# One-hots with four token columns side by side, a third place for x, stores issued ahead of loads

## The chip, the cores and the metric

The kernel runs on one core of one Trainium2 chip. The metric is the device time of one execution in microseconds (us), as the median of several runs. Of one execution there is a profile as well, taken by the hardware profiler. PE is TensorE's matmul, PEld its weight load, DVE is VectorE, ACT is ScalarE, POOL is GpSimd and SP is SyncE, which here only issues DMAs.

## What is computed

The reference has two parts. The first is a causal convolution over 8 batches of 3584 tokens with 192 features, 8 heads of 24 features and 7 taps per head (taps through a softmax). The second is a mixture of 8 experts on its result, 28672 tokens in all:

```
skip_score = x @ w_skip;  do_compute = skip_score > 0;  out = x.copy()
xc = x[do_compute];  logits = xc @ w_gate;  e_idx = argmax(logits)
gate_w = softmax(logits) at e_idx
for e in range(E):  h = max(xc[e_idx == e] @ w1[e], 0);  y = gate_w * (h @ w2[e])
out[do_compute] = xc + y
```

`w1[e]` is 192 x 1024, `w2[e]` is 1024 x 192.

## The kernel before, in words

**Stage 1: convolution and routing, by batch.** A batch is cut into 30 columns of 120 tokens (`NC = 30`, `R = 120`). `load_x(b)` fetches its 30 columns with 8 tokens of overlap into `xs`, 128 partitions wide, with three DMAs (four or more for the first two batches). `conv_head` (L331 to L340) makes one head: two matmuls of `toep` (the banded taps) with 15 columns of `xs` each into `pc`, which ACT copies into `ys` (L339). `pc` has two buffers, so two heads can run ahead of ACT. `ys` has two buffers too, by turns of the batches, and `store_y` writes it to `out`. `xs` has two buffers: even batches in one, odd ones in the other.

While batch b is convolved, batch b-1 is routed: `router` transposes `ys` on PE (`tp`, L423, copied by ACT to `ya`), multiplies with the router's weights (`pl`, `pb`) and leaves logits `lg`; `slots` finds on DVE the expert (`oh`), and by a matmul `pr` (L518) and a scan the slot of each token in its expert's list, as a row `rf` (0 to 127) and a column `qf` of a list of 128 x 144. Then `invert` (L575 on) turns slots into lists of tokens: for each column of 120 tokens it makes two one-hot matrices, `oa` (120 x 128, row of the slot, L606, times the column's token number `vtab`, L611) and `ob` (120 x 144, column of the slot, L617), and PE adds their product to `inv` (L589). DVE makes eight columns with one instruction each of `oa`, the product with `vtab`, and `ob`, so 30 columns are groups of 8, 8, 8 and 6. Before, `oa` is laid out `[R, P, IC]`, with the eight token columns innermost, and `ob` is `[R, IC, NQ]`, with the 144 list columns innermost and `qf` repeated along them.

**The weights of experts 0 and 1** are prepared in the same stage, as a background generator `split_weights`: 7 loads into `raw` (`w1` in one piece of 128 rows and two of 64, `w2` in four), 7 reductions on DVE for the largest value (`am`, L260), a scale, then 7 scalings on ACT to fp16 (`wt`, L279) and 7 subtractions on DVE for the low half (`wt`, L290). That is 26 steps an expert. `raw` has one buffer.

**What sets the order.** The order of instructions on each engine is the order in which the program writes them, and each engine and SP's queue handle theirs in that order; a scheduler moves nothing. In `phase1_step(b)` the eight heads are written one after another, and behind each head a table says how much else follows: `RR` steps of routing, `IR` steps of the inversion, `BGS[b][h]` steps of the background. Expert 0's steps are queued at batch 0, expert 1's at batch `E1`. After the last head comes `load_x(b + 2)`, and then `store_y(b)`. A load of `xs` waits until PE has finished with the batch that used the buffer; a copy into `ys` waits until the store of two batches ago has landed.

**Stage 2: the experts.** From the end of batch 7 on, blocks of 256 tokens are gathered from `out`, scaled, multiplied by `w1` (`ph`, L815), made into a high and low fp16 half (`hh` on ACT, L818; `hl` on DVE, L820), multiplied by `w2` (`po`) and scattered back. The first blocks take the lists of batches 0 to 4 and experts 0 and 1, while batches 6 and 7 are still routed and inverted beside them. `new_wt(e)` gives the weights' buffers: three by turns of `e % 3`.

## Time and profile before

| what | us |
|---|---|
| median of three runs | 716.0 |
| lowest and highest run | 714.67, 716.28 |
| the profiled execution | 714.31 |
| its span | 712.5 |
| PE busy | 666.1 (93%) |
| DVE busy | 580.2 (81%) |
| ACT busy | 319.6 (45%) |
| POOL busy | 399.5 (56%) |

The span runs from the first to the last instruction of the profiled execution. A row of instructions in order of time gives the start, the time, engine, line, operation, `out<-in` by the program's names, and in brackets how long the engine stood idle before it and for whom. A row of the groups gives line, engine, operation, shapes and count, then busy time, mean duration of one in ns, and idle time before. A recorded duration can overlap the start of the next instruction. Stretches give busy time of each engine, the clock granted to TensorE (1.00 is full), the mean busy share of the 16 DMA engines and what they moved. L117 and the like are lines of the kernel before.

### The profile page before, as it was taken

The numbers are of one execution on the slowest core, as the hardware profiler recorded it, in microseconds if no ns is written. First come the engines' busy times: TensorE is split into PE (matmuls) and PEld (weight loads), VectorE is DVE, ScalarE is ACT, GpSimd is POOL, SyncE is SP. The second block draws the span as 40 slices with busy tenths as digits, with TensorE's granted clock in tenths as the row PEclk, the third lists the DMA queues.
The fourth block names the chain that finished last, engine by engine and source line by source line (L and its number), as shares of the span: only waits on it lengthen the run. The fifth ranks groups of instructions, "written<-read, shape, count | busy, mean of one in ns | idle before, by whom it ended". The sixth has DMA issues, their size and how long they took to land.

```text
span 712.5 us, 16377 instructions
## 1 busy us (share of the span) xinstructions
PE 666.1 (93%) x5768; PEld 534.8 (75%) x5768; DVE 580.2 (81%) x1533; ACT 319.6 (45%) x654; POOL 399.5 (56%) x435
## 2 busy tenths in 40 slices
PE   4979699699999889999999999999999999999994
PEld 4646476466678889888888888888888888888883
DVE  4428679589899987998998998998998987777762
ACT  3646376367673223354363453543543533343321
POOL 4401020110750556777777777777777777777642
PEclk8998799799999999999999999999999999999997
DMA  7699889989495355466467357367465536999950
GB/s 227 204 263 291 235 235 287 249 202 268 114 224 180 84 128 130 110 163 150 130 171 171 89 168 181 89 159 170 125 181 118 166 84 182 268 315 267 314 171 12
DMA packets 158037, 129.59 MB, mean 182 GB/s; under 512 B 63238, under 2 KB 144904, under 8 KB 157946
## 3 DMA queue, kind: packets, MB, share of 16 engines
q1 hardware_dynamic: 143226, 106.59, 55.5%
q0 software_dynamic: 14720, 21.86, 12.3%
q8 instruction: 47, 0.77, 0.5%
q14 instruction: 44, 0.36, 0.2%
HBM read 69.76 MB, written 48.15 MB: 165 GB/s over the span
## 4 chain that ended last, share of the span: by engine, by line
PE 71%; DVE 13%; DMA 6%; issue 3%; SPq 2%; ACT 2%; POOL 2%; POOLq 0%; DVEq 0%; ACTq 0%
PE ph L815 33%; PE po L850 18%; PE po L853 9%; DMA out_dram<-ys 5%; PE pc L337 3%; DVE ob L617 3%; PE po L865 2%; PE tp L423 2%; SPq L390 2%; DVE oa L606 1%; DVE hl L820 1%; PE pp L350 1%; DMA raw<-in_moe_w_dram 1%; DVE oa L611 1%; DVE yt L789 1%
## 5 line engine op out<-in xcount | busy, mean ns | idle before, releaser
L818 ACT ACTIVATE hh<-ph 128x512 f16<-128x512 f32 x230 | 133.1, 590 | 226.5 <-PE ph L815 210.8
L815 PE MATMUL ph<-m,wt 128*128 128x256 f16 (+1 forms) x2000 | 220.4, 268 | 4.2 <-DVE hl L820 3.1
L815 PEld LDWEIGHTS <-wt 128*128 128x128 f16 x2000 | 188.7, 98 | 27.2 <-issue 5.0
L850 PE MATMUL po<-wt,hh 128*128 128x384 f16 x656 | 167.5, 326 | 0.0
L820 DVE SCALAR_TENSOR_TENSOR hl<-ph,hh 128x512 f16<-128x512 f32 x230 | 155.4, 685 | 11.1 <-ACT hh L818 9.9
L853 PE MATMUL po<-wt,hl 128*128 128x192 f16 x656 | 147.5, 246 | 0.0
L850 PEld LDWEIGHTS <-hh 128*128 128x128 f16 x808 | 78.3, 98 | 39.7
L770 POOL DMA_INDIRECT g<-gate_dr,sidx x82 | 87.4, 1066 | 25.0 <-issue 24.1
L839 POOL DMA_INDIRECT out_dram<-o,sidx x82 | 84.6, 1031 | 25.1 <-issue 6.4
L762 POOL DMA_INDIRECT y<-out_dram,sidx x82 | 83.9, 1023 | 25.3 <-issue 18.6
L853 PEld LDWEIGHTS <-hl 128*128 128x128 f16 x808 | 79.1, 98 | 10.2
L337 PE MATMUL pc<-xs,toep 128*120 128x360 f32 x224 | 82.1, 491 | 0.0
L836 DVE SCALAR_TENSOR_TENSOR o<-po,yf,y 128x192 f32<-128x192 f32 x115 | 47.3, 415 | 42.3 <-PE po L850 34.6
L784 ACT ACTIVATE yt<-y,ysc 128x192 f16<-128x192 f32 x115 | 46.4, 447 | 62.5 <-DVE ysc L314 52.9
L339 ACT COPY ys<-pc 120x720 f32<-120x720 f32 x56 | 42.6, 761 | 58.1 <-PE pc L337 33.5
L789 DVE SCALAR_TENSOR_TENSOR yt<-y,ysc,yt 128x64 f16<-128x64 f32 x230 | 58.3, 313 | 1.8 <-ACT yt L784 1.7
L337 PEld LDWEIGHTS pc<-xs,toep 128*120 128x120 f32 x224 | 38.3, 191 | 15.0 <-issue 2.0
L423 PE MATMUL tp<-ident,ys 120*128 120x120 f32 x240 | 33.1, 283 | 15.4 <-ACT ya L424 15.4
L260 DVE TENSOR_REDUCE am<-raw 128x1 f32<-128x512 f32 x56 | 37.8, 677 | 11.8 <-DMA raw<-in_moe_w_dram 11.5
L423 PEld LDWEIGHTS tp<-ident,ys 120*128 120x128 f32 x240 | 28.0, 149 | 25.7 <-ACT ya L424 17.7
L290 DVE SCALAR_TENSOR_TENSOR wt<-raw,ar,wt 128x512 f16<-128x512 f32 x56 | 41.8, 747 | 5.7 <-ACT wt L279 5.7
L836 DVE SCALAR_TENSOR_TENSOR o<-po,yf,o 128x192 f32<-128x192 f32 x101 | 42.2, 418 | 3.6
(197 smaller groups left out, 958.2 us busy)
## 6 DMA issues: line engine op xcount, KB each, us to landing
wd<-wscr SPq DMA_DIRECT2D x44, 449.0 KB
xs<-in_x_dram SPq DMA_DIRECT2D x6, 2688.0 KB
out_dram<-ys SPq DMA_DIRECT2D x6, 2610.0 KB
wscr<-wt SPq DMA_DIRECT2D x84, 128.0 KB
raw<-in_moe_w_dram SPq DMA_DIRECT2D x32, 192.0 KB
raw<-in_moe_w_dram SPq DMA_DIRECT2D x8, 512.0 KB
raw<-in_moe_w_dram SPq DMA_DIRECT2D x16, 256.0 KB
wscr<-wt SPq DMA_DIRECT2D x14, 256.0 KB
```

The costliest lines, as they stand in the source:

```text
L337: nc.tensor.matmul(pc[0:R, i, 0:n * G], toep[:, h, :], xs[:, c0 + n * i:c0 + n * i + n, h * G:(h + 1) * G], start=True, stop=True)
L423: nc.tensor.transpose(tp[:, u, :], src, ident[0:R, 0:R])
L762: rows_apart(nc.gpsimd.indirect_dma_start(out=k.y[:, u, :], out_offset=None, in_=out[0:k.rows, :], in_offset=bass.IndirectOffsetOnAxis(ap= ...
L770: nc.gpsimd.indirect_dma_start(out=k.g[:, u:u + 1], out_offset=None, in_=gate_dr[0:k.rows, :], in_offset=bass.IndirectOffsetOnAxis(ap=k.si ...
L789: nc.vector.scalar_tensor_tensor(out=yt[:, u, o:o + b_ - a], in0=k.y[:, u, a:b_], scalar=sc[:, u:u + 1], in1=yt[:, u, a:b_], op0=ALU.mult, ...
L815: nc.tensor.matmul(ph[:, f - f0, :], wt[:, o + f * P:o + (f + 1) * P], k.m[:, m, 0:w], start=(n == 0), stop=(n == len(seq) - 1))
L818: nc.scalar.activation(hh, ph, AF.Relu)
L820: nc.vector.scalar_tensor_tensor(out=k.hl[:, f0:f0 + fs, 0:w], in0=ph, scalar=0.0, in1=hh, op0=ALU.max, op1=ALU.subtract)
L836: nc.vector.scalar_tensor_tensor(out=o[:, u, :], in0=part, scalar=f2[:, u:u + 1], in1=base, op0=ALU.mult, op1=ALU.add)
L839: rows_apart(nc.gpsimd.indirect_dma_start(out=out[0:k.rows, :], out_offset=bass.IndirectOffsetOnAxis(ap=k.si[:, u:u + 1], axis=0), in_=o[: ...
L850: nc.tensor.matmul(po, k.hh[:, f, u * P:(u + 1) * P], w2[:, f], start=(f == 0), stop=(f == NF - 1))
L853: nc.tensor.matmul(po[:, 1], k.hl[:, f, u * P:(u + 1) * P], w2[:, f, 0], start=False, stop=False)
```

## The change

Four things are changed together.

**One-hots.** `IL = 4` replaces the two layouts by one. `oa` becomes `[R, 2, P, 4]` and `ob` `[R, 2, NQ, 4]`: two groups of four token columns, with the four columns innermost. A new helper `each` issues the DVE instruction for the two whole groups of four (or one, in the last group of six), and another for what is left, so that six columns take one instruction for four and one for two. The tables of indices are widened to match: `iota_r` from 8 to 4 copies, `iota_q` from one to 4. PE reads one column with a step of 4 elements from either. The branch that made `ob` on GpSimd, which was switched off, is gone.

**A third place for x.** The two weight buffers of `e % 3` 0 and 1 become one tile `wpair`, and its memory first holds batch 2's x. `XBUF` says which place each batch uses, and `XNEXT` which batch is loaded after which: x2 right after x1, x3 after batch 0, x4 after batch 1, x5, x6 and x7 after batches 3, 4 and 5.

**Stores ahead of loads.** After the last head of a batch `store_y(b)` comes first and the load second.

**Weights later.** `BGS` gets a row of zeros in front, so that expert 0's steps run in batches 2 to 4 (before 1 to 3), and `E1` is 4 instead of 3.

```
-BGS = ("00000000", "11111110", "11112222", "11112222") + ("11111111",) * 4
+BGS = ("00000000",) * 2 + ("11111110", "11112222", "11112222") + ("11111111",) * 3
 PICK = "102"
-E1 = 3
+E1 = 4
+
+XBUF = (0, 1, 2, 0, 1, 0, 1, 0)
+XNEXT = {0: 3, 1: 4, 3: 5, 4: 6, 5: 7}
...
+IL = 4
...
-    xp[1] = xodd.enter_context(tc.tile_pool(name="xp1", bufs=1, side="right"))
-    xp[0] = xeven.enter_context(tc.tile_pool(name="xp0", bufs=1, side="right"))
+    xp[0] = xlast.enter_context(tc.tile_pool(name="xp0", bufs=1, side="right"))
+    xp[1] = xfirst.enter_context(tc.tile_pool(name="xp1", bufs=1, side="right"))
...
+    wpair = wst.tile([P, 2 * WW], F16, tag="wt", bufs=1, name="wpair")
...
-        xs = xp[b % 2].tile([P, NC, D], F32, tag="xs", name=f"xs{b}")
+        if XBUF[b] < 2:
+            xs = xp[XBUF[b]].tile([P, NC, D], F32, tag="xs", name=f"xs{b}")
+        else:
+
+            xs = wpair.bitcast(F32)[:, 0:NC * D].rearrange("p (c d) -> p c d", d=D)
...
     xs[1] = load_x(1)
+    xs[2] = load_x(2)
...
-        return wst.tile([P, WW], F16, tag="wt", bufs=2, name=f"wt{e}")
+        return wpair[:, e % 3 * WW:(e % 3 + 1) * WW]
...
+        def each(out, in0, t, c0, op):
+
+            full = min(IC, NC - c0) // IL
+            n = out.shape[2]
+            for g0, g1, w in ((0, full, IL), (full, full + 1, min(IC, NC - c0) - full * IL)):
+                if g1 > g0 and w:
+                    src = in0[:, g0:g1, :, 0:w] if in0 is out else \
+                        in0[0:R, :, 0:w].unsqueeze(1).broadcast_to([R, g1 - g0, n, w])
+                    c = c0 + g0 * IL
+                    nc.vector.tensor_tensor(
+                        out=out[:, g0:g1, :, 0:w], in0=src, op=op,
+                        in1=t[0:R, c:c + (g1 - g0) * w].rearrange("p (g v) -> p g v", v=w).unsqueeze(2)
+                        .broadcast_to([R, g1 - g0, n, w]))
...
-            oa = wk1.tile([R, P, IC], F16, tag="oa", bufs=3, name=f"oa{b}_{c0}")
-            ob = wk1.tile([R, IC, NQ], F16, tag="ob", bufs=3, name=f"ob{b}_{c0}")
...
+            oa = wk1.tile([R, IC // IL, P, IL], F16, tag="oa", bufs=3, name=f"oa{b}_{c0}")
+            ob = wk1.tile([R, IC // IL, NQ, IL], F16, tag="ob", bufs=3, name=f"ob{b}_{c0}")
+            each(oa, iota_r, rf, c0, ALU.is_equal)
...
+            each(oa, oa, vtab, c0, ALU.mult)
...
+            each(ob, iota_q, qf, c0, ALU.is_equal)
...
-        if b + 2 < B:
-            xs[b + 2] = load_x(b + 2)
         if b < B - 2:
             store_y(b, ys[b])
+        if b in XNEXT:
+            xs[XNEXT[b]] = load_x(XNEXT[b])
```

What this makes of the order is shown at three places. The first is SP's queue behind the load of x1 (`out_0_dram<-ys0` is the store of batch 0, `raw0` the weights of expert 0). Before:

```order
L122 DMA xs1_161<-in_x_dram 112x192
L116 DMA xs2_340<-in_x_dram 120x192
L119 DMA xs2_340<-in_x_dram 128x28x192
L122 DMA xs2_340<-in_x_dram 112x192
L387 DMA out_0_dram<-ys0_229 120x29x192
L390 DMA out_0_dram<-ys0_229 104x192
L246 DMA raw0_367<-in_moe_w1_dram 128x1024
L249 DMA raw0_367<-in_moe_w1_dram 64x1024 x2
L252 DMA raw0_367<-in_moe_w2_dram 128x2x192 x4
L116 DMA xs3_508<-in_x_dram 120x192
L119 DMA xs3_508<-in_x_dram 128x28x192
```

Now, from x2's main piece on (which goes to `wpair`):

```order
L128 DMA wpair_91<-in_x_dram 128x28x192
L131 DMA wpair_91<-in_x_dram 112x192
L397 DMA out_0_dram<-ys0_235 120x29x192
L400 DMA out_0_dram<-ys0_235 104x192
L125 DMA xs3_347<-in_x_dram 120x192
L128 DMA xs3_347<-in_x_dram 128x28x192
L131 DMA xs3_347<-in_x_dram 112x192
L397 DMA out_0_dram<-ys1_353 120x29x192
L400 DMA out_0_dram<-ys1_353 104x192
L125 DMA xs4_507<-in_x_dram 120x192
L128 DMA xs4_507<-in_x_dram 128x28x192
L256 DMA raw0_546<-in_moe_w1_dram 128x1024
```

Store and load have changed places, each load is a batch further ahead, and expert 0's weights stand behind x4 instead of ahead of x3.

The second place is DVE's queue where the reductions of expert 0's weights (`am0`) begin: in batch 2 before, in batch 3 now. Before, no one-hot has been made yet:

```order
L509 SCALAR_TENSOR_TENSOR km0_544<-lg0_353,km0_544 120x30
L513 TENSOR_TENSOR oh0_547<-kq0_542,km0_544 120x30x8
L256 MEMSET am0_549 128x8
L260 TENSOR_REDUCE am0_549<-raw0_367 128x1
L522 TENSOR_REDUCE sm0_574<-ex0_540 120x30
L524 TENSOR_SCALAR sm0_574<-sm0_574 120x30
L527 RECIPROCAL gt0_577<-sm0_574 120x30
```

Now the same reduction stands within the last group of batch 0's inversion:

```order
L523 TENSOR_TENSOR oh1_785<-kq1_780,km1_782 120x30x8
L607 TENSOR_TENSOR oa0_24_787<-iota_r_195,rf0_628 120x512
L607 TENSOR_TENSOR oa0_24_787<-iota_r_195,rf0_628 120x128x2
L607 TENSOR_TENSOR oa0_24_787<-oa0_24_787,vtab_197 120x512
L607 TENSOR_TENSOR oa0_24_787<-oa0_24_787,vtab_197 120x128x2
L266 MEMSET am0_797 128x8
L270 TENSOR_REDUCE am0_797<-raw0_546 128x1
L532 TENSOR_REDUCE sm1_822<-ex1_778 120x30
L534 TENSOR_SCALAR sm1_822<-sm1_822 120x30
L537 RECIPROCAL gt1_825<-sm1_822 120x30
L607 TENSOR_TENSOR ob0_24_788<-iota_q_196,qf0_630 120x576
L607 TENSOR_TENSOR ob0_24_788<-iota_q_196,qf0_630 120x144x2
```

It is ahead of `ob0_24`, whose products PE has between batch 3's third and fourth head. The pieces of four columns (120x512, 120x576) and of two (120x128x2, 120x144x2) are seen here too.

The third place is DVE's queue where the fifth inversion ends (`inva` is the copy of its result). Now the first of expert 1's seven subtractions (`wpair<-raw1,ar1,wpair`) follows it, and the other six come further on, between the steps of batch 5's routing and behind them:

```order
L637 COPY inva_230<-inv_90 128x144
L300 SCALAR_TENSOR_TENSOR wpair_91<-raw1_1253,ar1_1662,wpair_91 128x512
L927 TENSOR_TENSOR tid_227<-inva_230,brow_228 128x2x7
L928 TENSOR_TENSOR cmp_226<-stab_214,cnta_224 128x2x7
L930 SCALAR_TENSOR_TENSOR sidxa_231<-cmp_226,tid_227 128x14
L503 TENSOR_REDUCE lm5_1930<-lg5_1590 120x30
L505 TENSOR_TENSOR lg5_1590<-lg5_1590,live_201 120x1
L507 TENSOR_TENSOR df5_1933<-lg5_1590,lm5_1930 120x240
```

Before, all seven stand ahead of it, in batch 6, between the instructions of that inversion; its end with the last two of the seven:

```order
L290 SCALAR_TENSOR_TENSOR wt1_772<-raw1_991,ar1_1394,wt1_772 128x512
L606 TENSOR_TENSOR oa4_16_1811<-iota_r_189,rf4_1729 120x1024
L611 TENSOR_TENSOR oa4_16_1811<-oa4_16_1811,vtab_191 120x1024
L617 TENSOR_TENSOR ob4_16_1812<-iota_q_190,qf4_1731 120x1152
L290 SCALAR_TENSOR_TENSOR wt1_772<-raw1_991,ar1_1394,wt1_772 128x512
L606 TENSOR_TENSOR oa4_24_1845<-iota_r_189,rf4_1729 120x128x6
L611 TENSOR_TENSOR oa4_24_1845<-oa4_24_1845,vtab_191 120x128x6
L617 TENSOR_TENSOR ob4_24_1846<-iota_q_190,qf4_1731 120x864
L631 COPY inva_224<-inv_90 128x144
```

So these seven have gone from batch 6 to batch 7. PE's own order is the same as before.

More of the change, by code (lines that the diff above doesn't have):

```diff
@@ L609, in invert @@
             yield
-            if not by_gpsimd:
-                nc.vector.tensor_tensor(out=oa[:, :, 0:ic], in0=oa[:, :, 0:ic], in1=bm(vtab[0:R], P), op=ALU.mult)
+            each(oa, oa, vtab, c0, ALU.mult)
             products(at)
@@ L614, in invert @@
             yield HOP
-            columns(IC // 2)
-            if not by_gpsimd:
-                nc.vector.tensor_tensor(out=ob[:, 0:ic, :], in0=iota_q[0:R].unsqueeze(1).broadcast_to([R, ic, NQ]),
-                                        in1=qf[:, c0:c0 + ic].unsqueeze(2).broadcast_to([R, ic, NQ]), op=ALU.is_equal)
+            each(ob, iota_q, qf, c0, ALU.is_equal)
             products(at)
-            due.extend((at + lag, c0, v0, oa, ob) for v0 in (0, IC // 2))
+            due.extend((at + lag, c0, i, oa, ob) for i in range(IC // IL))
             at += 1
```

39 lines of the change are left out of this document (13 added, 26 removed).

## The prediction

> **What bounds the kernel now.** I read the times by stretch first: the convolution stage by batch, the start of the expert stage, and the rest.
>
> ```profile
> core 0 of [0], span 712.5 us
> core 0: us, PE busy (x) PEld busy (x) DVE busy (x) ACT busy (x) POOL busy (x), PEclk, DMA share, GB/s
> 24.30:28.50 4.20, 4.20 (x15) 2.48 (x15) 1.07 (x4) 2.28 (x3) 0.00 (x0) 1.00 0.01 4
> 28.50:180.40 151.90, 132.46 (x951) 92.18 (x949) 106.20 (x219) 87.08 (x187) 19.60 (x31) 0.91 0.91 250
> 180.40:260.00 79.60, 72.19 (x709) 60.43 (x708) 75.63 (x192) 37.74 (x86) 38.45 (x41) 0.98 0.58 152
> 46.20:73.10 26.90, 22.95 (x152) 15.79 (x151) 20.70 (x43) 13.72 (x30) 4.24 (x7) 0.87 1.01 266
> 73.10:104.10 31.00, 24.47 (x168) 17.25 (x166) 20.85 (x45) 17.17 (x37) 3.05 (x5) 0.83 0.85 234
> 104.10:125.70 21.60, 20.86 (x168) 14.72 (x166) 21.15 (x43) 13.10 (x30) 3.61 (x5) 1.00 1.00 280
> 125.70:155.80 30.10, 24.06 (x167) 16.71 (x166) 20.41 (x45) 13.65 (x31) 3.04 (x6) 0.83 0.88 228
> 155.80:180.40 24.60, 22.43 (x182) 15.77 (x180) 23.09 (x46) 16.97 (x38) 3.17 (x8) 1.00 0.85 238
> ...
> 320.00:712.00 392.00, 382.84 (x3383) 314.12 (x3380) 328.71 (x890) 158.15 (x308) 284.12 (x278) 0.99 0.64 168
> ```
>
> The five middle rows are batches 2 to 6, cut at each batch's first matmul. Batch 4, which nothing disturbs, takes 21.6 us; batches 2, 3 and 5 take 26.9, 31.0 and 30.1 at a granted clock of 0.83 to 0.87; batch 6 takes 24.6 with DVE at 23.09. The excess over five times 21.6 is 26.2 us, the ceiling for this stage. From 180.4 to 260 DVE is the bound (75.63 of 79.6); from 320 on it is PE (382.84 of 392), so what is won before 260 should stay won. Next, what PE waited for in the long batches, from PE's instructions in order of time and the list of waits:
>
> ```profile
> 53.54 1.86 PE L423 MATMUL tp<-ident,ys 120*128 120x120 f32 x8 [3.95 <-ACT ya L424]
> 83.39 1.86 PE L423 MATMUL tp<-ident,ys 120*128 120x120 f32 x8 [6.53 <-ACT ya L424]
> 104.09 1.42 PE L337 MATMUL pc<-xs,toep 128*120 128x360 f32 x4
> 107.67 0.98 PE L423 MATMUL tp<-ident,ys 120*128 120x120 f32 x8
> 112.38 0.55 PE L589 MATMUL inv<-ob,oa 120*128 120x144 f16 x6
> 134.18 1.86 PE L423 MATMUL tp<-ident,ys 120*128 120x120 f32 x8 [4.75 <-ACT ya L424]
> 137.33 0.36 PE L518 MATMUL pr<-oh,ones 120*128 120x240 f16 x1 [1.29 <-DVE oh L513]
> ...
> ACT ys L339 <- DMA out_dram<-ys: 21.9, 4, 8.5
> ```
>
> PE stands still after two heads of batches 2, 3 and 5, because ACT may not copy into a `ys` buffer whose store has not landed. After each such stop eight transposes take 1.86 us instead of 0.98, so a stop costs some 2.5 us beyond its length. The store is late because of its place in SP's queue, whose issues in order of time are:
>
> ```profile
> 28.55 0.35 SPq L116 DMA_DIRECT2D xs<-in_x_dram  x1
> ...
> 35.00 0.39 SPq L387 DMA_DIRECT2D out_dram<-ys  x1
> ```
>
> Batch 0 is done at about 28.5, yet its store goes out at 35.0 behind the load of x2. The load could not start earlier either, since x2 used batch 0's buffer: that is why the DMA share is 0.01 from 24.3 to 28.5. From there on the queue is nearly full (0.91, 250 GB/s).
>
> **The change, part by part. 1: queue and buffers.** The queue carries these pieces (KB each):
>
> ```profile
> xs<-in_x_dram SPq DMA_DIRECT2D x6, 2688.0 KB
> out_dram<-ys SPq DMA_DIRECT2D x6, 2610.0 KB
> raw<-in_moe_w_dram SPq DMA_DIRECT2D x32, 192.0 KB
> raw<-in_moe_w_dram SPq DMA_DIRECT2D x8, 512.0 KB
> raw<-in_moe_w_dram SPq DMA_DIRECT2D x16, 256.0 KB
> xs<-in_x_dram SPq DMA_DIRECT2D x8, 90.0 KB
> xs<-in_x_dram SPq DMA_DIRECT2D x8, 84.0 KB
> out_dram<-ys SPq DMA_DIRECT2D x8, 78.0 KB
> ```
>
> A load of one batch is 2688+90+84 = 2862 KB (2.93 MB), a store 2688 KB (2.75 MB), an expert's weights 512+2x256+4x192 = 1792 KB (1.84 MB). Six loads (x2 to x7), six stores (y0 to y5) and two experts make 37.8 MB; the window 28.5 to 180.4 moved 151.9 x 0.250 = 38.0 MB. So before batch 7 starts, just this has passed. In the new order the same 37.8 MB stand ahead of batch 7, only x7 is now the last of them, behind y5, and batch 7's first matmul needs x7. They can start at 24.3, because x2 has a place of its own. So the queue decides: at 250 GB/s x7 lands at 24.3+151.2 = 175.5; at 266 and 280 GB/s, the two windows with a share of 1.0, at 166.4 and 159.3. PE alone would allow 46.2+5x21.6 = 154.2.
>
> I take 256 GB/s, nearer to the lower end, because PE still stops twice. Walking through at that rate (a load 11.4, a store 10.8, weights 7.2 us): x2 lands at 35.7, y0 46.5, x3 57.9, y1 68.7, x4 80.1, expert 0's weights 87.3, y2 98.0, y3 108.8, x5 120.2, five of seven pieces of expert 1 125.8, y4 136.6, x6 148.0, the other two 149.5, y5 160.3, x7 171.7. PE: batch 2 runs 46.2 to 67.8 without a stop, since y0 is away at 46.5. In batch 3 something new comes: its first reduction of the weights on DVE now stands ahead of the last `ob` of the inversion, and it waits for weights that were moved behind x4. How DVE stands in such a wait is to be seen before:
>
> ```profile
> 55.67 0.69 DVE L260 TENSOR_REDUCE am<-raw 128x1 f32<-128x512 f32 x1 [4.46 <-DMA raw<-in_moe_w_dram]
> ...
> 133.49 0.69 DVE L260 TENSOR_REDUCE am<-raw 128x1 f32<-128x512 f32 x1 [7.02 <-DMA raw<-in_moe_w_dram]
> ```
>
> The first 0.52 MB land at 80.1+2.0 = 82.1, the `ob` follows by my estimate 1.7 us later (the reduction takes 0.69, and three small instructions stand between), and PE would have been there about 9 us into the batch (8.3 in batch 4, 104.09 to 112.38): a stop of 7 us, and 2.5 for the clock. Batch 3 ends at 98.9, about when y2 has landed, so the queue loses 1 us at most. Batch 4 ends at 120.5 (x5 there at 120.2), batch 5 at 142.1; then PE waits for x6 until 148.0, pays 2.5 again, and with batch 6 relieved of the weights' work (21.6 instead of 24.6) ends at 172.1. Batch 7 starts at 172, not 180.4: **8.4 us**, between 4.9 (queue at 250) and 16.
>
> **2: one-hots.** DVE's instructions by form, in 180.4 to 260, then the weights' work of batch 6, then an `ob` as the chain that ended last counts it:
>
> ```profile
> L617 DVE TENSOR_TENSOR ob<-iota_q,qf 120x1152 f16<-120x1152 f16 x9 | 12.1, 1346 | 0.0
> L606 DVE TENSOR_TENSOR oa<-iota_r,rf 120x1024 f16<-120x1024 f16 x9 | 6.3, 704 | 0.0
> L611 DVE TENSOR_TENSOR oa<-oa,vtab 120x1024 f16<-120x1024 f16 x9 | 6.2, 692 | 0.3
> L617 DVE TENSOR_TENSOR ob<-iota_q,qf 120x864 f16<-120x864 f16 x3 | 3.2, 1051 | 0.0
> L611 DVE TENSOR_TENSOR oa<-oa,vtab 120x768 f16<-120x768 f16 x3 | 1.7, 555 | 0.1
> ...
> L290 DVE SCALAR_TENSOR_TENSOR wt<-raw,ar,wt 128x512 f16<-128x512 f32 x6 | 4.5, 744 | 0.0
> ...
> 101.88 1.27 DVE ob L617
> ```
>
> `oa`, with adjacent columns innermost in all operands, takes about half of `ob`'s time per element. Its two forms give (692-555)/256 = 0.535 ns per element and 144 ns fixed (some 80 ns of that overlap the next instruction: in the chain an `ob` counts 1.27). With four columns innermost I take the same rate for `ob`: 760 ns, 586 less. The group of six columns becomes four and two: `ob` 452+298-80 = 670, 381 less; `oa` and its product 0.06 more each. In the DVE-bound stretch: 9x0.586+3x0.381-6x0.06 = 6.0 us less.
>
> [...]
>
> **3: expert 1's weights.** Its seven subtractions (L290) and five scalings by ACT leave batch 6 and come after batch 5's inversion, in batch 7: 7x(0.744-0.08) = 4.7 us for DVE. In the stretch DVE idles for 4.0 us (79.6-75.63), and I count half of that as filled by this work. Net: 6.0-4.7 of work less and 2.0 of idle time used: **3 us**, between 0 and 5.
>
> **4: without a price.** The weights read by the inversion's products now stand 8 bytes apart instead of 16, the columns 8 instead of 2. Weights at 16 bytes already load as fast as adjacent ones:
>
> ```profile
> L589 PEld LDWEIGHTS <-oa 120*128 120x128 f16 x240 | 22.2, 147 | 7.3 <-issue 6.4 <-DVE ob L617 0.4
> L520 PEld LDWEIGHTS <-um 120*120 120x120 f16 x8 | 1.2, 146 | 0.2
> ```
>
> So I take nothing. If the moving side took twice its time (0.06 us, four products in 0.42), 90 products of the stretch would cost PE 5.4 us, of which its 7.4 us idle hide most. The index tables on GpSimd have 1088 elements instead of 1168, in batch 0 off the path.
>
> **Sum.** 8.4+3 = 11.4 us off the profiled execution's 714.3 (its span is 712.5), 702.9. That execution lay 1.7 below the median of the runs, 716.0; as a median I expect 704.6. A measurement can tell 0.2% (1.4 us) from no change.
>
> **Rivals.** (a) *The queue gains only its idle gap*: rate 250, and expert 1's work eats the one-hots' gain. For it: three of five windows run below 240 GB/s, and the weights' waits move rather than go. 716-4.9 = 711; chance 0.15. (b) *The queue runs full*: at 268 GB/s x7 lands at 165 and batch 3's stop is short: 716-16-2 = 698; chance 0.10; against it, weights still arrive while DVE waits for them. (c) *`ob` is not sped up*: four adjacent columns are no better than none. Then the stretch gains nothing and takes 4.7 more less 2.0 of idle: -8.4+2.7, about 710; chance 0.04; `oa` speaks against it. (d) *Won time is given back*: the end hangs on something with a clock of its own, such as DMA of the expert stage; 716, chance 0.05; PE's 382.84 of 392 speaks against it. (e) *Slower*: short rows cost `oa` and its product their double rate, so that they go at `ob`'s present one. 1024 elements then take about 1.2 us, 0.53 more; the stretch gets 9x2x0.53+3x2x0.4 = 12 us, and expert 1's 4.7 less 2 idle, +15; the batches get 4 us of DVE work each, where DVE has 0.45 idle of 21.6, so that about half of the 8.4 is lost too: 716+15-4 = 727, or 721 if `ob` still gains its 6; I say 722. It decides from about 0.3 us more per `oa` instruction (24 of them in the stretch against 3+4). For it: no row has runs as short as 8 bytes; against: runs of 16 and 12 bytes go at one rate. Chance 0.09.
>
> **Numbers.** The forecast, 0.57, stands at 704.6. Cases with (a), (b) and (c) reach from 698 to 711, with the bounds of parts 1 and 3 to 713; (d) and (e), 0.14, stay outside. Faster by over 0.2%: 0.57+0.15+0.10+0.04 = 0.86; the same: 0.05; slower: 0.09.
>
> **To be seen afterwards.** Right: `ob` near 0.76 us recorded; x2's load at once behind x1's; no stop in batch 2, one of 5 to 8 us in batch 3 behind DVE's `am`, one at the first head of batch 6 for x6; batch 7 from 170 to 174; what stands at 260 before near 249. Wrong: `ob` above 1 us, a DMA share under 0.9 from 24 to 172, or batch 7 starting after 177; or gains up to 260 that are gone at the end.

## The result, and the profile after

The changed kernel took 719.22 us (median of 6 runs), the kernel before 715.34 (6 runs on the same chip): the ratio is 1.0057, with a 95% interval of 1.0036 to 1.0079. A second measurement gave 718.62 against 714.45, 1.0061 (1.0037 to 1.0084). So the change costs 0.6%, some 4 us, where 704.6 was forecast. One of the six runs took 1761.17 us, far above the others, and the ratio leaves it out. The profiled execution took 719.6; its span is 717.9, 5.4 more than before.

The stretches of the changed kernel, those that answer to the rows shown of before: the gap at the start, batch 7 up to the place that stood at 260, batches 2 to 6, and the expert stage.

```profile
core 0: us, PE busy (x) PEld busy (x) DVE busy (x) ACT busy (x) POOL busy (x), PEclk, DMA share, GB/s
24.30:28.50 4.20, 3.77 (x18) 2.85 (x18) 1.55 (x5) 1.74 (x3) 1.31 (x5) 1.00 1.09 320
...
186.35:265.50 79.15, 75.31 (x708) 63.12 (x706) 74.00 (x207) 41.69 (x94) 36.54 (x43) 1.00 0.54 151
49.74:70.99 21.25, 20.73 (x152) 14.43 (x151) 13.76 (x33) 14.07 (x32) 2.61 (x5) 1.00 0.93 252
70.99:104.31 33.32, 24.11 (x166) 17.03 (x165) 19.52 (x51) 13.01 (x29) 3.24 (x6) 0.85 0.88 229
104.31:132.54 28.23, 22.61 (x167) 16.05 (x165) 24.76 (x58) 16.96 (x36) 3.37 (x5) 0.95 0.91 237
132.54:160.42 27.88, 24.56 (x164) 17.33 (x165) 14.13 (x33) 13.29 (x29) 2.48 (x4) 0.93 0.93 244
160.42:186.35 25.93, 25.93 (x178) 18.79 (x179) 18.49 (x54) 13.54 (x30) 2.03 (x5) 0.94 0.80 213
325.40:717.40 392.00, 383.27 (x3386) 314.46 (x3383) 329.33 (x891) 157.95 (x308) 285.28 (x278) 0.99 0.64 168
```

The idle gap of the DMA engines is filled (share 1.09 where it was 0.01), and the expert stage is what it was (392.00 us with PE at 383.27, before 382.84). All of the loss is there when batch 7 starts: 186.35, not 180.4. By batches: batch 2 starts 3.5 us later than before (49.74 against 46.20), then batch 2 is 5.6 shorter, batch 3 is 2.3 longer, batch 4 is 6.6 longer, batch 5 is 2.2 shorter and batch 6 is 1.3 longer, together +6.0. From there to the old 260 it wins 0.5. What PE waits for, from its instructions in order of time (only those rows):

```profile
20.10 4.34 PE L360 MATMUL pp<-xs,toep 128*120 128x360 f32 x10 [2.69 <-POOL toep L201]
...
31.93 1.37 PE L347 MATMUL pc<-xs,toep 128*120 128x360 f32 x4
...
88.19 0.95 PE L595 MATMUL inv<-ob,oa 120*128 120x144 f16 x6 [9.21 <-DVE ob L607]
...
132.54 2.73 PE L347 MATMUL pc<-xs,toep 128*120 128x360 f32 x4 [5.62 <-DMA xs<-in_x_dram]
...
160.42 2.72 PE L347 MATMUL pc<-xs,toep 128*120 128x360 f32 x4 [3.32 <-DMA xs<-in_x_dram]
```

There is no stop for a store any more in batch 2. There are four others: the bands `toep` come late before batch 1, batch 3 stands 9.2 us behind DVE, batch 5 waits for x5 and batch 6 for x6. The stop in batch 3 on DVE:

```profile
86.24 0.69 DVE L270 TENSOR_REDUCE am<-raw 128x1 f32<-128x512 f32 x1 [10.63 <-DMA raw<-in_moe_w_dram]
...
87.74 0.61 DVE L607 TENSOR_TENSOR ob<-iota_q,qf 120x576 f16<-120x576 f16 x2
```

The groups of the one-hots (DVE), and of their products (PE):

```profile
L595 PE MATMUL inv<-ob,oa 120*128 120x144 f16 x240 | 39.8, 307 | 9.2 <-DVE ob L607 9.2
...
L607 DVE TENSOR_TENSOR ob<-iota_q,qf 120x1152 f16<-120x1152 f16 x24 | 18.0, 749 | 0.0
...
L607 DVE TENSOR_TENSOR oa<-oa,vtab 120x1024 f16<-120x1024 f16 x24 | 16.6, 692 | 0.8
...
L607 DVE TENSOR_TENSOR ob<-iota_q,qf 120x288 f16<-120x288 f16 x8 | 2.4, 302 | 0.0
```

`ob` takes 749 ns instead of 1346, as forecast, and `oa` stays at 692. The products did not stay: 307 ns recorded for one where 233 stood. Eight and four in a row, first before, then after:

```profile
177.31 0.69 PE L589 MATMUL inv<-ob,oa 120*128 120x144 f16 x8
...
195.12 0.42 PE L589 MATMUL inv<-ob,oa 120*128 120x144 f16 x4
```

```profile
64.84 0.69 PE L595 MATMUL inv<-ob,oa 120*128 120x144 f16 x4
...
155.88 1.22 PE L595 MATMUL inv<-ob,oa 120*128 120x144 f16 x8
```

Four of them take 0.42 before and 0.69 now, so that a further one costs (0.69-0.42)/4 = 0.067 us then and (1.22-0.69)/4 = 0.132 now: twice the time with columns 8 bytes apart. Over 240 products that is 16 us more of PE.

### The profile page after: what moved, and what is told of

Its sections match the earlier page's. It is cut to its first block, busy times and chain, and to the rows that moved or that the text cites. A ratio compares the mean times of both kernels' runs of the same rounds, so it can differ in the third digit from the quotient of the medians.

```text
span 717.9 us, 16404 instructions
## 1 busy us (share of the span) xinstructions
PE 674.9 (94%) x5768; PEld 542.2 (76%) x5768; DVE 563.7 (79%) x1557; ACT 319.6 (45%) x654; POOL 396.7 (55%) x435
## 4 chain that ended last, share of the span: by engine, by line
PE 65%; DVE 4%; issue 0%; ACT 0%; POOL 0%; POOLq 0%; DVEq 0%
PE ph L821 34%; PE po L856 18%; PE po L859 9%; PE po L871 2%; PE tp L433 1%; DVE hl L826 1%; PE inv L595 1%; DVE oa L607 1%; DVE ob L607 0%; DVE o L842 0%; PE pl L446 0%; DVE yt L795 0%; DVE yam L785 0%; DVE oh L523 0%; PE pl L450 0%
## 5 line engine op out<-in xcount | busy, mean ns | idle before, releaser
L821 PE MATMUL ph<-m,wpair 128*128 128x256 f16 (+1 forms) x1520 | 166.3, 267 | 1.0 <-ACT ys L349 0.9
L821 PEld LDWEIGHTS <-wpair 128*128 128x128 f16 x1520 | 142.8, 98 | 18.4 <-issue 1.8
L856 PE MATMUL po<-wpair,hh 128*128 128x384 f16 x464 | 118.5, 326 | 0.0
L859 PE MATMUL po<-wpair,hl 128*128 128x192 f16 x464 | 104.3, 246 | 0.0
L347 PE MATMUL pc<-xs,toep 128*120 128x360 f32 x192 | 70.5, 491 | 8.9 <-DMA xs<-in_x_dram 8.9
L821 PE MATMUL ph<-m,wt 128*128 128x256 f16 x480 | 54.4, 273 | 0.0
L821 PEld LDWEIGHTS <-wt 128*128 128x128 f16 x480 | 47.0, 98 | 5.9
L347 PEld LDWEIGHTS pc<-xs,toep 128*120 128x120 f32 x192 | 33.9, 196 | 23.1 <-issue 11.6
L856 PE MATMUL po<-wt,hh 128*128 128x384 f16 x192 | 49.0, 326 | 0.0
L595 PE MATMUL inv<-ob,oa 120*128 120x144 f16 x240 | 39.8, 307 | 9.2 <-DVE ob L607 9.2
```

The lines of the kernel that those rows point to most:

```text
L347: nc.tensor.matmul(pc[0:R, i, 0:n * G], toep[:, h, :], xs[:, c0 + n * i:c0 + n * i + n, h * G:(h + 1) * G], start=True, stop=True)
L595: nc.tensor.matmul(inv, oa[:, i, :, v], ob[:, i, :, v], start=(b in (0, REL + 1) and w == 0), stop=(b in (REL, B - 1) and w == NC - 1))
L821: nc.tensor.matmul(ph[:, f - f0, :], wt[:, o + f * P:o + (f + 1) * P], k.m[:, m, 0:w], start=(n == 0), stop=(n == len(seq) - 1))
L856: nc.tensor.matmul(po, k.hh[:, f, u * P:(u + 1) * P], w2[:, f], start=(f == 0), stop=(f == NF - 1))
L859: nc.tensor.matmul(po[:, 1], k.hl[:, f, u * P:(u + 1) * P], w2[:, f, 0], start=False, stop=False)
```

## The experiments

The sets were run on several chips. In the first, second and fifth set every kernel took some 130 us longer, the kernel before too (842.3, 854.1, 849.7 us), nearly all of it in the expert stage; of these sets only the ratio to their own runs of before and the batches' starts are used. In the third and fourth the kernel before took 714.5 and 716.0. In the table "after" is the changed kernel and "before" the kernel before, whose batch 7 starts at 180.4.

| set | kernel | ratio to before (95%) | batch 7 starts |
|---|---|---|---|
| 1 | after, one-hots as before | 1.0072 (1.0032-1.0112) | 184.8 |
| 1 | before, one-hots with 4 columns | 0.9987 (0.9954-1.0020) | 183.0 |
| 1 | after, 2 columns | 1.0053 (1.0020-1.0087) | 186.4 |
| 1 | after, x2's memsets on DVE | 1.0118 (1.0077-1.0159) | 185.3 |
| 2 | before, one-hots with 2 columns | 0.9924 (0.9887-0.9960) | 179.3 |
| 2 | after, expert 0's loads earlier | 1.0034 (1.0004-1.0065) | 184.7 |
| 2 | after, loads first | 0.9980 (0.9950-1.0010) | 179.4 |
| 2 | after, four repairs | 0.9938 (0.9906-0.9970) | 177.4 |
| 3 | after again | 1.0061 (1.0037-1.0084) | 187.1 |
| 3 | after, more background in batches 5, 6 | 1.0070 (1.0054-1.0086) | 190.4 |
| 3 | before, weights later alone | 1.0066 (1.0045-1.0088) | 180.6 |
| 3 | after, loads first, 2 columns, more background | 0.9878 (0.9860-0.9895) | 180.1 |
| 4 | before, one-hots with 4 columns | 0.9929 (0.9901-0.9957) | 183.3 |
| 4 | before, one-hots with 2 columns | 0.9899 (0.9869-0.9929) | 180.7 |
| 4 | after, loads first | 0.9960 (0.9943-0.9977) | 177.8 |
| 4 | after, loads first, 2 columns | 0.9888 (0.9863-0.9913) | 175.0 |
| 5 | before, stores first alone | 1.0115 (1.0069-1.0162) | 188.7 |
| 5 | loads first, 2 columns, memsets on DVE | 0.9969 (0.9934-1.0004) | 175.3 |

**One-hots.** First undone in the changed kernel (the old `invert` and its index tables), then done alone in the kernel before:

> The changed kernel with the one-hots laid out as before; third place, order of stores and later weights stay. Theory P (the four-column layout makes PE's inversion products slower, 0.69 us for four in place of 0.42, and that eats what DVE wins): four products are back at 0.42, ob at 1.35 us, the stretch from batch 7's start to the place that stood at 260 loses 6 us on PE and gets 6 us back on DVE, the time stays within 2 us of the changed kernel's 719.2 (717 to 721). Rival D (DVE's gain was real and the loss lies only in the queue): the time rises by 5 us or more, to 724 to 727.

> The kernel before with the new one-hots alone. Theory P: ob 0.75 us, four products 0.69; PE gets 0.067 x 240 = 16 us more work, 6 of it in the stretch from 180 to 260, where DVE loses 6 of 75.6 of its work and PE then has 78 of 79.6: 1 to 2 us won there; up to 2 us lost in each batch that is not standing still for a store. Together 715 to 718, against 715.3 before. Rival D (the products hide behind DVE and the queue): 4 to 6 us faster, 710 to 711.

Undone, four products are back at 0.42 us and the time is the changed kernel's within the interval, as the products' price would have it; but the interval (1.0032 to 1.0112) also holds 4 us of loss. This run alone therefore decides nothing. Alone in the kernel before the one-hots gave 0.9987 in this set, and 0.9929 in set 4 (below), where the expert stage is not longer. Then the mechanism: two token columns side by side, products still by four.

```
-IL = 4
+IL = 2
...
-nc.tensor.matmul(inv, oa[:, i, :, v], ob[:, i, :, v], ...
+nc.tensor.matmul(inv, oa[:, v // IL, :, v % IL], ob[:, v // IL, :, v % IL], ...
```

> The changed kernel with two token columns side by side in place of four, so that the products read columns 4 bytes apart in place of 8; products still come four at a time. Theory P with a price that hangs on the distance: four products fall back towards 0.42 to 0.5 us, ob stays near 0.75, the time falls by 3 to 7 us, to 712 to 716. Rival S (any distance over 2 bytes costs the same): four products 0.69, time 719 as it is. Rival W (runs of one 4-byte word cost DVE its rate, so that only runs of two columns lose): ob at 1.3 us or more, oa too at 1.2, the time rises above 727.

The groups with two columns:

```profile
L595 PE MATMUL inv<-ob,oa 120*128 120x144 f16 x240 | 25.0, 233 | 10.8 <-DVE ob L607 10.2 <-DVE sl L558 0.6
...
L607 DVE TENSOR_TENSOR ob<-iota_q,qf 120x1152 f16<-120x1152 f16 x24 | 18.0, 749 | 0.0
L607 DVE TENSOR_TENSOR oa<-iota_r,rf 120x1024 f16<-120x1024 f16 x24 | 16.6, 692 | 0.0
```

Columns 4 bytes apart cost PE nothing (233, as with adjacent ones), and DVE takes the same 749 ns with two columns side by side as with four. So the price hangs on the distance: rivals S and W are out. Every run changed the distance of the weights (`oa`) together with that of the moving side (`ob`); that the moving side has the price is argued from the recorded weight loads, which were longest (147 ns) where the products were fast, and no run shows it alone. In the time of the changed kernel nothing of it is seen (1.0053, batch 7 at 186.4, where theory P had 712 to 716 us): there PE waits 8.0 us for x5 and 4.5 for x6, where it was 5.6 and 3.3. In the kernel before it is seen; set 2 and set 4:

> The kernel before with the one-hots alone, two token columns side by side in place of four; queue, places and weights as before. Theory P (four columns cost PE 0.067 us per product, two cost nothing; ob falls to 0.75 us either way): the stretch from batch 7's start on wins 4 to 6 us on DVE and loses nothing on PE: ratio 0.992 to 0.995 to the kernel before, where four columns alone gave 0.9987 on another chip. Rival Q (what DVE wins is taken up by waits for stores and weights): ratio 0.998 to 1.001.

> The kernel before with the new one-hots alone, four columns. Theory P (DVE wins 6 us after batch 7's start, PE pays 6 for its 90 products there and some 2 us in each batch without a stop): ratio 0.998 to 1.002. Rival D (the products hide): 0.992 to 0.994.

> The kernel before with the one-hots alone, two columns. Theory P (no price on PE, all of DVE's gain): ratio 0.990 to 0.994, 4 to 7 us below the four columns. Rival D: equal to the four columns within 1.5 us.

Four columns alone win 0.71%, 5.1 us of 716; two columns 1.01%, 7.2 us. The intervals overlap, so their difference, 2 us, is not settled here. The profiles say where it is: from batch 7's start to the last matmul four columns win 3.8 us (2.9 late, then 0.9 early), two win 5.5 (0.3 late, then 5.2 early). These are single executions (714.3, 713.0 and 708.9 us), of which the second lies 2.5 above the median of its kernel, so they say where more than how much. With loads first (below) the same step is 0.9960 against 0.9888, intervals apart, 5 us. So the price is 2 to 5 us, mostly hidden where PE waits anyway. For the four columns alone theory P had 0.998 to 1.002 and charged too much; 0.9929 lies in rival D's range.

**The late start.** The two memsets of the third place on VectorE:

```
+eng = nc.vector if b == 2 else nc.gpsimd
-nc.gpsimd.memset(xs[0:HALO, 0, :], 0.0)
-nc.gpsimd.memset(xs[96:P, NC - 1, :], 0.0)
+eng.memset(xs[0:HALO, 0, :], 0.0)
+eng.memset(xs[96:P, NC - 1, :], 0.0)
```

> The changed kernel with the two memsets of the third place's edge rows moved from GpSimd to VectorE, which does nothing then. Theory H (these two memsets push GpSimd's chain to toep back and PE then starts the heads late and at a lower clock): batch 1 starts at 28 to 29 in place of 31.9, batch 2 at 46 to 47 in place of 49.7, and 3.5 us are won to the end: 715 to 716.5. Rival L (the start is late for another reason, such as x2's transfer beside x0's and x1's): batch 1 still starts at 31 to 32 and the time stays at 719.

PE's ten matmuls that wait for the bands, and the start of batch 1:

```profile
18.23 2.65 PE L361 MATMUL pp<-xs,toep 128*120 128x360 f32 x10 [1.23 <-POOL toep L202]
...
28.42 1.37 PE L348 MATMUL pc<-xs,toep 128*120 128x360 f32 x4
```

The cause of the late start is shown: 28.42, as before the change (28.36). A gain is not: the ratio is 1.0118, no better than without the repair. Batch 3 starts 3.2 us sooner (67.8) and lasts 2.4 longer, since expert 0's weights land hardly sooner (its reduction runs at 85.65 in place of 86.24), and batch 7 comes at 185.3, 1.1 sooner. Theory H fell at the end of the chain.

**The weights' wait in batch 3.** Expert 0's seven loads go ahead of batch 1's store and x4; their use stays in batch 3.

```
-BGS = ("00000000",) * 2 + ("11111110", "11112222", "11112222") + ("11111111",) * 3
+BGS = ("00000000", "11111110", "00000000", "11112222", "11112222") + ("11111111",) * 3
```

> The changed kernel with the seven loads of expert 0's weights issued a batch earlier (in batch 1, ahead of batch 1's store and x4), their use left in batch 3. Theory Q (batch 3's stop of 9.2 us is DVE standing in the first reduction for weights queued behind x4, and the late end of batch 3 makes y3 and x5 late, which is the stop of 5.6 ahead of batch 5): no stop behind that reduction, batch 4 starts at 93 to 97 in place of 104.3, batch 5 at 122 to 126 in place of 132.5, batch 7 at 177 to 181 in place of 186.4, ratio 0.996 to 1.000 where the changed kernel has 1.0057. Rival B (bytes alone set the pace, so that a wait taken away here comes back at the next place): batch 7 still at 185 to 187, ratio 1.005.

PE's stops in order of time:

```profile
83.02 1.86 PE L433 MATMUL tp<-ident,ys 120*128 120x120 f32 x8 [7.09 <-ACT ya L434]
133.23 2.73 PE L347 MATMUL pc<-xs,toep 128*120 128x360 f32 x4 [5.65 <-DMA xs<-in_x_dram]
```

The stop behind DVE is gone, and in its place PE stands 7.1 us for the store y1, which the weights now delay. Batch 5 starts at 133.2, as with the wait (132.5), and batch 7 at 184.7. Rival B holds, nearly to its numbers: here a wait taken away came back at the next transfer.

**The order of store and load.** The two statements at the end of a batch change places, first in the changed kernel:

```
-        if b < B - 2:
-            store_y(b, ys[b])
         if b in XNEXT:
             xs[XNEXT[b]] = load_x(XNEXT[b])
+        if b < B - 2:
+            store_y(b, ys[b])
```

> The changed kernel with each load issued ahead of the store, as before. Theory O (from batch 3 on there are two places again, and a store of 14 us ahead of a load makes the next batch start late): no wait for x5 at batch 5 and for x6 at batch 6 (5.6 and 3.3 us), in their place waits of ACT for a store after two heads, shorter by some 2 to 4 us each; in batch 2 a stop of 2 to 4 us for y0, which stores ahead of loads had taken away. Batch 7 at 182 to 186, ratio 0.999 to 1.005. Rival N (the order is what took the stops of batch 2 away and is worth more than it costs): batch 7 after 187, ratio 1.007 or more.

> The changed kernel with loads ahead of stores, four columns. Theory O (stores ahead of loads make batches 5 and 6 start late, as x5 and x6 are needed at a batch's first head and a store's landing only after its second): batch 7 at 178 to 181 in place of 186.4 to 187.1, ratio 0.996 to 1.000 against 1.0061. Rival N (order is indifferent to the end): 1.004 or more.

Batches 4, 5 and 6 of set 4, and PE's stops:

```profile
100.50:122.90 22.40, 22.40 (x167) 16.13 (x166) 20.31 (x48) 16.96 (x36) 2.46 (x5) 1.00 0.95 269
122.90:145.30 22.40, 22.40 (x166) 16.11 (x165) 17.92 (x44) 13.08 (x29) 2.44 (x5) 1.00 1.01 273
145.30:177.80 32.50, 27.14 (x180) 19.30 (x179) 18.65 (x54) 13.66 (x29) 3.02 (x6) 0.89 0.78 211
```

```profile
58.26 1.34 PE L433 MATMUL tp<-ident,ys 120*128 120x120 f32 x8 [4.64 <-ACT ya L434]
81.72 1.09 PE L433 MATMUL tp<-ident,ys 120*128 120x120 f32 x8 [0.51 <-ACT ya L434]
152.63 1.09 PE L433 MATMUL tp<-ident,ys 120*128 120x120 f32 x8 [3.35 <-ACT ya L434]
```

Batch 2 stands for y0 again (4.6 us), batch 3 hardly, and batches 4 and 5 run through at 22.4 us each, where they took 28.2 and 27.9. Batch 6, which now starts 15 us sooner, gives 6.6 of that back, with a stop of 3.4 us for y4 and a lower clock (0.89). Batch 7 starts 8.6 us sooner, and the ratio is 0.9960 against 1.0061 of set 3, with intervals apart: the order is worth 1.0%, 7 us. Theory O holds. The same order alone in the kernel before, which has two places:

> The kernel before with each store issued ahead of the load that follows it, and nothing else. Theory O (a store takes 13 to 14 us at 190 to 200 GB/s, a load 9 at 310 to 330; with two places the load can go only when its batch is done, and behind the store it lands 23 us later, after PE's 21.6 us for a batch): PE waits for x at the first head of most batches, batch 7 at 184 to 190, ratio 1.005 to 1.015. Rival N (the order moves the stops from the third head to the first and no more): batch 7 at 179 to 182, ratio 0.998 to 1.002.

The list of its PE waits up to batch 7:

```profile
PE pc L337 <- DMA xs<-in_x_dram: 29.2, 6, 11.8
```

Six starts of a batch wait for x, 29.2 us in all, and batch 7 starts at 188.7, 8.3 later. Theory O holds here too (1.0115). This shows without the third place that the order costs.

**Weights a batch later.** In the kernel before the table and `E1 = 4` alone; then the changed kernel with `"11112222"` for batches 5 and 6 too:

> The kernel before with the weights of experts 0 and 1 a batch later and nothing else. Theory A: batch 2 loses the stop behind expert 0's weights but not the one for y0; expert 1's work in batch 7 costs 3 to 6 us (DVE is the bound of that stretch with the old one-hots): ratio 1.003 to 1.008, batch 7 at 178 to 181. Rival K: the weights move from one full stretch of the queue to another and nothing changes, 0.999 to 1.002.

> The changed kernel with four more background steps in batch 5 and four in batch 6, so that expert 1's scalings on ScalarE and subtractions on VectorE are done before batch 7. Theory A (in batch 7 PE waits for ScalarE's copies, queued behind expert 1's scalings, and for VectorE: the 3.2 us by which the changed kernel falls behind between the start of batch 7 and its last head): the five or six scalings of 0.73 us are gone from batch 7, and batch 7's last head comes 2 to 3 us sooner after its first, 0.996 to 0.998 of the changed kernel's time. Rival K (the work costs batch 6 what it spares batch 7): batch 7 starts 2 to 3 us later and the sum stays.

From batch 7's start to the first `ph`, in the kernel before, with the weights later, and with more background:

```profile
180.40:201.95 21.55, 19.98 (x149) 13.51 (x148) 19.02 (x59) 15.37 (x36) 17.35 (x24) 1.00 0.53 138
```

```profile
180.60:206.50 25.90, 20.65 (x149) 13.48 (x148) 23.39 (x65) 19.50 (x44) 20.84 (x31) 1.00 0.48 127
```

```profile
190.40:211.60 21.20, 20.66 (x149) 14.00 (x148) 17.85 (x59) 15.63 (x39) 17.08 (x25) 1.00 0.51 135
```

Weights later alone cost 0.66%, 4.7 us, as theory A said. Batch 7 still starts on time (180.6), and 4.35 are lost in its first 26 us, where DVE has 4.4 us more to do and ACT 4.1. The two longest of PE's waits there:

```profile
196.43 0.43 PE L454 MATMUL pb<-ident,lt 128*120 128x128 f32 x2 [0.74 <-ACT lt L444]
200.97 1.03 PE L436 MATMUL pl<-ya,wra 128*32 128x240 f32 x16 [1.34 <-ACT lg L457]
```

Both are for ACT's small copies of the router. What holds up the first of them, `lt`, from the rows of DVE and ACT:

```profile
193.77 0.75 DVE L290 SCALAR_TENSOR_TENSOR wt<-raw,ar,wt 128x512 f16<-128x512 f32 x1
194.43 0.16 DVE L314 TENSOR_SCALAR ysc<-yam 128x2 int32<-128x2 int32 x1
...
194.68 0.80 ACT L784 ACTIVATE yt<-y,ysc 128x192 f16<-128x192 f32 x2 [1.84 <-issue]
...
196.02 0.36 ACT L444 COPY lt<-pl 128x240 f32<-128x240 f32 x1
```

ACT stands idle for 1.84 us ahead of `yt`, which needs `ysc` from DVE, and `ysc` stands behind one of expert 1's subtractions. The copy `lg` stands behind the next `yt` in the same way (1.51 us idle). So it is DVE's queue that sets these waits, by way of ACT. DVE itself idles 2.53 us of this stretch before (21.55-19.02) and 2.51 with the weights later (25.90-23.39): the work went into the time in full. In the changed kernel the stretch takes 24.84 with DVE at 22.32, again 2.52 idle. A wait of 0.72 us, for `gr`, does follow one of ACT's scalings of 0.73 us; the two engines' parts were not measured one without the other.

With more background batch 7's stretch is back at 21.20, but it starts 3.4 later than in the changed kernel of the same set: DVE now meets the last weights of expert 1 in batch 5, and PE stands for `ob` behind it:

```profile
163.20 1.21 PE L595 MATMUL inv<-ob,oa 120*128 120x144 f16 x8 [6.10 <-DVE ob L607]
```

The sum stays (1.0070), as rival K said, by another way than it said.

**The changed kernel again, and the versions put together.** The one with four repairs has the memsets on DVE, expert 0's earlier loads, two columns, and this end of a batch:

```
+        if b < B - 2 and b < 3:
+            store_y(b, ys[b])
         if b in XNEXT:
             xs[XNEXT[b]] = load_x(XNEXT[b])
+        if 3 <= b < B - 2:
+            store_y(b, ys[b])
```

The others put the edits shown above together: loads first, two columns and more background; the same without more background; and that with the memsets on DVE.

> The changed kernel itself once more, beside the runs of the kernel before on the same chip as the three others, since the variants ran on another chip than the first pair. Ratio to the kernel before 1.003 to 1.010 by either theory (1.0057 on the first chip); batch 7 at 185 to 187.

> All repairs in one: edge rows of the third place on VectorE, expert 0's loads a batch earlier, stores ahead of loads in batches 0 to 2 and loads ahead of stores from batch 3 on, two token columns side by side. Theory (the four causes are the start, the products, the wait for the weights and the late x5 and x6, and they add up): batch 2 at 46, batch 4 at 90 to 94, batch 7 at 172 to 177, four products 0.42 us; ratio 0.980 to 0.986 to the kernel before. Rival B (the transfers' bytes at 200 GB/s for stores and 320 for loads are the bound, so that the stage cannot end before batch 7 at 178 to 180): ratio 0.990 to 0.993.

> The changed kernel with loads ahead of stores, two token columns side by side, and the denser background of batches 5 and 6. Theory (order, products and batch 7's background work add up): batch 7 at 177 to 179 as in the run with loads first less some of the products' 2 us a batch, ratio to the kernel before 0.988 to 0.992, below the one-hots alone with two columns (0.9924). Rival B (the third place gives nothing that the order of the transfers does not give back): 0.992 to 0.995.

> The changed kernel with loads ahead of stores and two columns, without the denser background of batches 5 and 6. Theory (the stop of 12.7 us that the denser background put at the end of batch 5 goes, and expert 1's work costs 3 to 4 us in batch 7 instead): batch 6 at 142 to 144, batch 7 at 175 to 179, ratio 0.986 to 0.990, 5 to 8 us below loads first with four columns. Rival (the denser background was what made it fast): ratio 0.991 or more.

> Loads ahead of stores, two columns, and the two memsets of the third place's edge rows on VectorE. Theory H: batch 1 starts at 28 to 30 in place of 31.9, of which 1 to 3 us are left at batch 7: ratio 0.984 to 0.988, against 0.9888. Rival B (the queue takes the earlier start back in batch 2's and batch 3's stops): batch 7 at 174 to 176, ratio 0.988 to 0.990.

The four repairs at once gave 0.9938, just past rival B's end: the causes do not add up. Loads first with two columns and more background gave 706.35 us, 0.9878, though it stands 12.7 us at the end of batch 5:

```profile
155.29 1.12 PE L595 MATMUL inv<-ob,oa 120*128 120x144 f16 x8 [12.67 <-DVE ob L607]
```

Without the additional background it gave 707.42, 0.9888: batch 6 starts at 141.7 in place of 156.2, but stands 7.2 us for y4 in batch 6, and batch 7 starts at 175.0, 5 us sooner, of which expert 1's work in batch 7 takes most. A batch without a stop takes 20.60 us in it:

```profile
99.30:119.90 20.60, 20.60 (x167) 14.60 (x165) 19.30 (x44) 16.90 (x37) 2.44 (x5) 1.00 0.93 265
```

The memsets on DVE add nothing there (batch 7 at 175.3; the time's ratio, 0.9969, is from a set with the longer expert stage). The two ratios with loads first and two columns (0.9878 and 0.9888) and that of two columns alone in the kernel before (708.56, 0.9899) have intervals that overlap: with loads first, the third place and the later weights together neither win nor lose anything that shows.

## Why the prediction was wrong

**The gap and the third place.** "x2's load at once behind x1's" and "no stop in batch 2" came true. That this is won time did not. The loads bring two memsets each, and x2's stand on GpSimd ahead of the bands:

```profile
10.40 0.25 POOL L123 MEMSET wpair<- 8x192 f32 x1
10.69 0.25 POOL L124 MEMSET wpair<- 32x192 f32 x1
```

The prediction followed the load on SP's queue alone and left these out. GpSimd reaches the bands' chain 1.8 us later (0.6 of it the memsets, 0.8 a copy of `hist` that took 1.19 us in place of 0.35, and some tenths in smaller steps). With the memsets on VectorE the chain is back in its time (the first of its `toep` at 17.74; before the change 17.68, after it 19.61), so that the longer copy went with them; why stays open. PE waits 2.69 us, and its next ten matmuls then take 4.34 us in place of 2.65. That is the 3.6 us at batch 1. It costs the end little: of the 3.5 us which its repair won at the start, 1.1 were left at batch 7, and with loads first none.

**The walk-through of the queue: the step that failed.** It is "Batch 4 ends at 120.5 (x5 there at 120.2)". The store y3 and the load x5 behind it were counted at 10.8 and 11.4 us, 22.2 together, so that x5 was there in time by 0.3 us. In the run the two took 28.2 us, from batch 3's end to the first matmul of batch 5, and PE waited 5.6 of them, so that batch 4 took 6.6 us more than its 21.6. Batch 7 started 14.3 us after the forecast 172: these 6.6 are the largest part, 3.5 more came with the late start, 2.2 in batch 3 and 2 in batches 5 and 6. The wait for x6 was foreseen. "I take 256 GB/s" for both directions gave the two halves wrongly, though their sum nearly rightly. Stretches of the changed kernel with only a load, only a store, a load again, and the end of that load:

```profile
73.00:80.50 7.50, 5.98 (x39) 4.50 (x37) 2.53 (x8) 5.24 (x10) 0.93 (x1) 1.00 1.10 337
...
105.00:117.00 12.00, 12.00 (x82) 8.90 (x84) 11.69 (x35) 9.78 (x19) 1.14 (x2) 1.00 0.83 193
121.00:129.00 8.00, 5.91 (x48) 3.67 (x46) 7.15 (x14) 3.84 (x12) 1.54 (x3) 1.00 1.09 334
129.00:133.00 4.00, 0.46 (x1) 0.48 (x2) 2.26 (x6) 0.00 (x0) 0.00 (x0) 0.58 1.06 246
```

and of the kernel before, a store and a load:

```profile
70.00:79.00 9.00, 6.86 (x57) 4.51 (x49) 7.66 (x17) 1.75 (x6) 1.75 (x4) 1.00 0.83 198
108.00:117.50 9.50, 8.76 (x74) 6.11 (x72) 9.22 (x25) 5.80 (x11) 0.93 (x1) 1.00 1.09 322
```

A load of 2.93 MB takes 2.93/0.334 = 8.8 us, a store of 2.75 MB 2.75/0.193 = 14.2. A mean over a stretch with both hid this, and with it what the order does: with the store first x5 cannot be there for 23 us, with the load first it is there after 9. From batch 3 on there are two places again, because the third is full of weights. A load can then start only when its batch is done, and it has until the end of the next batch, 21.6 to 22.6 us. Behind the store that is 14.2+8.8 = 23.0. The other 5 of the 28.2 us were priced at nothing: by an estimate from the stretches, 1 us until the store's bytes flow, 1 at the change from one to the other, and 3 at the end, where expert 1's first weights, issued behind x5, share the queue (the row from 129 to 133); no run shows these 5 apart. With the load first x5 is there in time, and the store has two more heads (some 4 us) before ACT needs its buffer. That is the 7 us which the experiments found. They changed the order in all batches; that the gain lies in batches 4 and 5 is read from their stops. Stores first, which the prediction counted as a gain in batch 2, moved that stop to the weights in batch 3.

**The stop in batch 3** was foreseen, at its place and for its reason: 9.2 us where 7 were said, since batch 3 began 3.2 later, the weights came 4 later (86.2 against 82.1) and PE needed the `ob` 1 us earlier in the batch.

**The one-hots** were right in DVE's part: 749 ns for 760, and with two columns 5.5 us won from batch 7 on, where 6.0 were said. "I take nothing" for the products was the error, and the bound beside it ("if the moving side took twice its time") gave the size: 0.065 us more each, 0.132 us a product with columns 8 bytes apart against 0.065 to 0.067 with 4 and 2. Which side has the price no run shows alone. That most of it hides was half right: 2 to 5 us show, in a batch without a stop 1.8 (22.40 with four columns, 20.60 with two). The two-column piece of the last group, whose pairs lie 8 bytes apart, took 302 ns, where the prediction's rate gives 0.535x288+144 = 298.

**Expert 1's weights** were priced at 4.7 us of DVE less 2 of idle, 2.7. Alone they cost 4.7 of the median. The 2 us of idle time were the error: DVE's idle time up to the first `ph` stayed at 2.5 us, and its additional work went into the time in full. ACT's scalings, six of 0.74 us in the stretch, were named and got no price; the runs do not separate them. From batch 7 to the old 260 the change won 0.5 us, where 3 were forecast.

**The sum**, in ratios to before: one-hots -5.1 us, weights later +4.7, order +7.2; with +4.3 measured, -2.5 are left for the third place. This takes it that the parts add up, though the order was measured in the changed kernel and the other two in the kernel before. That last is a remainder and was not measured alone, since the third place lies in the weights' buffers and can't be had without the later weights. The forecast had -8.4 for queue, place and order together (+4.7 by this count) and -3 for one-hots and weights (-0.4). Of the rivals none was it: (e) had the right sign, but by DVE's rate, which held, and its 722 was near by chance; (d)'s giving back at the end did not happen, the expert stage is unchanged. Of (a) one reason was seen, that the weights' waits move rather than go. Its upper case (b) has a slip: from 180.4 to 165 is 15 us and not 16.

## What to carry to other kernels

Price loads and stores from stretches that hold only one of them, and then ask of each order what is needed first: a transfer on which the next batch's first instruction waits belongs ahead of one that is only needed to free a buffer. When a layout is changed for the engine that writes it, price the engine that reads it at the new distance (here 0.132 us a product in place of 0.067), and give the price a term of its own even where it seems hidden. And where a queue is full, expect a stop that is taken away to come back at the next transfer in it: here the 9.2 us behind the weights came back as 7.1 for the store y1, and only the order changed its end.

## What the runs showed of the hardware

- A store of 768-byte rows from 120 partitions ran at 193 to 198 GB/s with a DMA share of 0.83, a load of such rows at 322 to 337 with 1.09 to 1.10, in the stretches of both kernels shown above.
- A product in fp16 with 144 moving columns: 0.065 to 0.067 us for a further one at 2 and 4 bytes' distance of the columns, 0.132 at 8 (the weights at 16, 4 and 8). The recorded weight loads beside it went the other way than feared: 147 ns with columns 16 bytes apart, 117 with 8, 102 with 4.
- DVE makes 1152 elements of fp16 in 749 ns whether the innermost run has four elements or two, and 288 in 302 ns where two of every four are taken.
- The ten matmuls after the 2.69 us wait at the start ran at a granted clock of 0.60 (before the change 1.00), the column before the DMA share:

```profile
20.10:24.40 4.30, 4.30 (x10) 2.47 (x10) 4.23 (x10) 1.30 (x2) 4.14 (x6) 0.60 1.10 314
```
In two other runs (the four repairs, and loads first with two columns and the memsets on DVE) they took 4.10 and 4.28 us after a wait of only 0.54 and 0.55, in the kernel before with stores first alone 2.65 after 0.55, so that the wait alone does not decide it; this stays open.
